# Routing of a mixture of experts: wide operations on groups of tiles, rank split by shift and mask, gathers of the uncertain slots moved into their branches

## The chip, the cores and the metric

The kernel runs on one core of a Trainium2 chip. The metric is the device time of one execution in microseconds (us). The engines are TensorE (PE, and PEld for its weight loads), VectorE (DVE), ScalarE (ACT), GpSimd (POOL) and SyncE (SP), which issues most DMAs.

## The reference

Linear attention over 4 batches, 8 heads, 768 positions and 48 dimensions gives 3,072 tokens of 384 values. Each token goes to one of 8 experts, the one with the highest logit, and the output of this expert's two layers is scaled by a gate:

```python
state = alpha[:, :, t, :, None] * state + einsum('bhd,bhe->bhde', k[:, :, t], v[:, :, t])
y[:, :, t] = einsum('bhd,bhde->bhe', q[:, :, t], state)
...
logits = x @ w_gate + modality_bias[modality_id]
e_idx = argmax(logits, axis=1)
probs = softmax(logits);  gate_w = probs[arange(N), e_idx]
for e in range(8):
    h = maximum(x[e_idx == e] @ w1[e], 0)          # 384 -> 1024
    out[e_idx == e] = gate_w[..., None] * (h @ w2[e])  # 1024 -> 384
```

## The kernel before, in words

**Attention.** The tokens are 24 tiles of 128, called chunks. A loop runs over the chunks in a software pipeline: `decay` (L229) makes the scans G and Fw on VectorE, `scale` (L254) the products kh and qh (L257, L260), `scores` (L263) the score matmuls (L269), and `combine` (L284) carries the state: t = S*G on VectorE (L292), its copy UB by ScalarE (L295), the state's matmuls kv (L301), and the output matmuls y (L314 with UB, L316 with the scores), copied to yt by ScalarE (L318). `rows` (L321) transposes yt and stores the tokens in DRAM (`xd`); `logits` (L332) does the logits of two chunks at once and adds the bias table bt (L347).

**Routing.** `route_group` (L388) runs after chunks 5, 11, 15, 17, 21 and 23, for groups of 6, 6, 4, 2, 4 and 2 tiles. Per group: the highest logit mx; per tile eq, which marks the highest logits by a descending number (L395); m2 and the one-hot oh (L397); matmuls with a triangle of ones and with all ones, which count for each token how many tokens of its expert come before it (L399 to L405, in PSUM tile rp); per tile the rank r1, as a sum over rj (L407); ohs, the running sum of oh (L412, L415); per tile hr, the rank divided by 128, as a count of thresholds not above it (hj, L417); hi (a key of expert and hr) and lo (the rest of the division); per tile OL (L423), which holds the token's number at column lo. `route_early` (after chunks 15 and 17) picks the experts of slots 0 and 1 and starts their weights and gathers. `route_end` (L524) counts the tokens of each expert (the count matmul, L529 to L531), lays out the remaining slots, and forms with OH (L558) and OL in a matmul (the table, L565) the list of tokens of each slot.

**Experts.** A slot is 256 tokens of one expert; 12 slots always exist (NS0 = 12). Weights are split into two parts for exact products (w1H, w1L, w2H, w2L, L775 and L777), as are the tokens (xL, L769) and the hidden values (hL, L802). GpSimd gathers the tokens of a slot (`gather`, L605) and their gates (`gather_gates`, L610) and scatters the results (`put`, L748). Slots 12 to 18 are uncertain: `tail(i)` (L872) enters slot i if ns > i (L874), and does a full slot if nfl > i, else one of 128 tokens (`half`). In both cases `ahead_of(i + 1)` (L866) starts weights and gathers of the next slot first. For these inputs ns is 13 and slot 12 is a half one, so slot 13 is not entered. Behind the tail a flag is tested (L908) for inputs out of range, which is not taken; then two puts write tile `of`, slot 12's result.

**Order.** Queues are in order. The order of the instructions on each engine is set when the kernel is built, by a scheduler that simulates the engines; a change of one instruction can therefore move others. An `If` that isn't taken is a jump on each engine, and the skipped side brings the engine's semaphores up to date (EVENT_SEMAPHORE, and INC_SWDGE_SEM for GpSimd's DMA queue, named ISA in the order), which on GpSimd waits for its DMAs in flight.

Of the kernel before, what the change touches and what calls it, by code (L numbers as in the profile page):

```python
# [21 lines left out]
P = 128  # L22
# [5 lines left out]
E = 8  # L28
# [3 lines left out]
NU = N // P  # L32
# [22 lines left out]
def attention_moe(ctx: ExitStack, tc: tile.TileContext, q, k, v, alpha, mid, wg, mb, w1, w2, out):  # L55
    nc = tc.nc
# [130 lines left out]
    pool.memset(ones, 1.0)  # L187
    tri = cp.tile([P, P], BF16, name="tri")
    pool.affine_select(tri, ones, [[1, P]], ALU.is_gt, 0.0, base=0, channel_multiplier=-1)
    thr = cp.tile([P, NU - 1], F32, name="thr")  # L190
    pool.tensor_scalar(thr, iof[:, 1:NU], float(P), None, op0=ALU.mult)
    onh = cp.tile([P, NU - 1], F32, name="onh")
    pool.memset(onh, 1.0)
# [138 lines left out]
    def logits(i, after=None):  # L332

        lt = ps.tile([P, 2, P], F32, name="kv")
        with issue_after(after):
            for j in range(NP):
                mark["logitst"] = pe.matmul(
                    lt[32 * j : 32 * j + 32], wgp[:, j], st[i, "yt"][:, :, j], start=True, stop=True
                )
        ls = sb.tile([P, 2, P], F32, name="lts")  # L340
        mark["xc"] = act.copy(ls, lt)
        lp = ps.tile([P, 2, P], F32, name="kv")
        for c in range(2):
            mark["logits"] = pe.transpose(lp[:, c], ls[:, c], ident)
        z = slice(i - 1, i + 1)
        vec.tensor_reduce(L[:, z], lp.rearrange("p c (j e) -> p c e j", e=32)[:, :, :E], axis=AX.X, op=ALU.add)
        vec.tensor_tensor(L[:, z], L[:, z], bt[:, z], op=ALU.add)  # L347

    def logits_pe(i, xs, pl):
        xt = ps.tile([P, ND, P], F32, name="tr", bufs=3)  # L350
        for c in range(ND):
            pe.transpose(xt[:, c], xs[:, c * P : (c + 1) * P], ident)
        xc = pl.tile([P, ND, P], F32, name="xc")
        act.copy(xc, xt)
        lp = ps.tile([P, E], F32, name="kv")
        for c in range(ND):
            pe.matmul(lp, xc[:, c], wgs[:, c], start=(c == 0), stop=(c == ND - 1))
        vec.tensor_tensor(L[:, i], lp, bt[:, i], op=ALU.add)

    mx = cp.tile([P, NU], F32, name="mx")
# [11 lines left out]
    key0 = cp.tile([P, 2], F16, name="key0")  # L373
    OHE = cp.tile([P, EARLY[-1], 2], F16, name="OHE")
    rj = cp.tile([P, E], F32, name="rj")
    hj = cp.tile([P, NU - 1], F32, name="hj")
    hr = cp.tile([P, NU], F32, name="hr")
    r1 = cp.tile([P, NU], F32, name="r1")
    lo = cp.tile([P, NU], F32, name="lo")
    OL = cp.tile([P, NU, P], F16, name="OL")  # L380
    meta = cp.tile([1, NS + 2], I32, name="meta")
    idx = cp.tile([P, NH], I32, name="idx")
# [5 lines left out]
    def route_group(t0, t1):  # L388
        n = t1 - t0
        s = slice(t0, t1)  # L390
        sh = [P, n, E]

        vec.tensor_reduce(mx[:, s], L[:, s], axis=AX.X, op=ALU.max)
        for t in range(t0, t1):
            vec.scalar_tensor_tensor(eq[:, t], L[:, t], mx[:, t : t + 1], rev, op0=ALU.is_equal, op1=ALU.mult)  # L395
        vec.tensor_reduce(m2[:, s], eq[:, s], axis=AX.X, op=ALU.max)
        vec.tensor_tensor(oh[:, s], eq[:, s], m2[:, s].unsqueeze(2).broadcast_to(sh), op=ALU.is_equal)  # L397
        rp = ps.tile([P, n, E], F32, name="rt")
        pe.matmul(rp, tri, oh[:, s], start=True, stop=False)  # L399
        for t in range(t0, t1 - 1):  # L400
            m = t1 - 1 - t
            pe.matmul(
                rp[:, t + 1 - t0 :], ones, oh[:, t].unsqueeze(1).broadcast_to([P, m, E]), start=False, stop=False
            )
        mark["rank"] = pe.matmul(rp, ones, ohs.unsqueeze(1).broadcast_to(sh), start=False, stop=True)  # L405
        for t in range(t0, t1):
            vec.scalar_tensor_tensor(  # L407
                rj, rp[:, t - t0], 1.0, oh[:, t], op0=ALU.mult, op1=ALU.mult, accum_out=r1[:, t : t + 1]
            )
        if t1 == NU and n > 1:  # L410
            vec.tensor_reduce(hsum, oh[:, t0 : t1 - 1].rearrange("p t e -> p e t"), axis=AX.X, op=ALU.add)
            vec.tensor_tensor(ohs, ohs, hsum, op=ALU.add)  # L412
        elif t1 < NU:
            vec.tensor_reduce(hsum, oh[:, s].rearrange("p t e -> p e t"), axis=AX.X, op=ALU.add)
            vec.tensor_tensor(ohs, ohs, hsum, op=ALU.add)  # L415
        for t in range(t0, t1):
            vec.scalar_tensor_tensor(  # L417
                hj, thr, r1[:, t : t + 1], onh, op0=ALU.is_le, op1=ALU.mult, accum_out=hr[:, t : t + 1]
            )
        vec.scalar_tensor_tensor(hi[:, s], m2[:, s], -float(NU), hr[:, s], op0=ALU.mult, op1=ALU.add)  # L420
        vec.scalar_tensor_tensor(lo[:, s], hr[:, s], -float(P), r1[:, s], op0=ALU.mult, op1=ALU.add)
        for t in range(t0, t1):
            vec.tensor_scalar(OL[:, t], ioh, lo[:, t : t + 1], tok[:, t : t + 1], op0=ALU.is_equal, op1=ALU.mult)  # L423

    nj = cp.tile([P, E, 2, NS0], F32, name="nj")
    nn = cp.tile([P, 2, E], F32, name="nn")
# [53 lines left out]
    def route_early(s):  # L480
# [14 lines left out]
        else:  # L495
# [28 lines left out]
    def route_end(na):  # L524
# [30 lines left out]
        for g in range(3):  # L555
            n = NU // 3
            z = slice(g * n, (g + 1) * n)
            vec.tensor_tensor(  # L558
                OH[:, z, :nh],
                key[:, :nh].unsqueeze(1).broadcast_to([P, n, nh]),  # L560
                hi[:, z].unsqueeze(2).broadcast_to([P, n, nh]),
                op=ALU.is_equal,
            )
            for t in range(g * n, (g + 1) * n):
                mark["table"] = pe.matmul(tp, OL[:, t], OH[:, t, :nh], start=(t == 0), stop=(t == NU - 1))  # L565
        for m, g in ((NS, NG), (NS + 1, E)):
            vec.tensor_scalar(meta[:, m : m + 1], beg[0:1, g : g + 1], float(na), float(NS), op0=ALU.add, op1=ALU.min)
        return places(tp, slice(z0, NH))

    ls = cp.tile([P, NU, E], F32, name="ls")  # L570
    sm = cp.tile([P, NU], F32, name="sm")
    gt = cp.tile([P, NU], F32, name="gt")

# [11 lines left out]
    def gates(t0, t1):  # L585
        z = slice(t0, t1)
        sh = [P, t1 - t0, E]
        vec.tensor_tensor(ls[:, z], L[:, z], mx[:, z].unsqueeze(2).broadcast_to(sh), op=ALU.subtract)
        act.activation(ls[:, z], ls[:, z], AF.Exp)
        vec.tensor_reduce(sm[:, z], ls[:, z], axis=AX.X, op=ALU.add)  # L590
        vec.tensor_scalar(sm[:, z], sm[:, z], 1e-9, None, op0=ALU.add)
# [159 lines left out]
    def experts(ahead):  # L751
# [114 lines left out]
        def ahead_of(i):  # L866
            if i < NS:
                weights(i, i % 2)
                gather(i)
                gather_gates(i)  # L870

        def tail(i):  # L872
            if i < NS:
                with tc.If(ns > i):  # L874
                    if i > NS0:
                        prep(i)
                    with tc.If(nfl > i) as full:
                        ahead_of(i + 1)
                        act.copy(XH[i % 2], xf)
                        vec.tensor_tensor(XL[i % 2], xf, XH[i % 2].bitcast(F32), op=ALU.subtract)  # L880
                        slot(i)
                    with full.Else():
                        ahead_of(i + 1)
                        half(i)
                    tail(i + 1)
# [59 lines left out]
```

## Time and profile before

| | |
|---|---|
| median of 3 runs | 447.57 us (447.39 to 449.25) |
| profiled execution | 447.26 us, of which the span of the trace is 445.4 |
| mean granted TensorE clock | 0.965 |
| PE | busy 396.4 us (89% of the span) |
| DVE | busy 276.3 us (62%) |
| ACT | busy 234.7 us (53%) |
| POOL | busy 139.6 us (31%) |

Attention and the routing beside it take the first 192 us or so, a transition with the last routing group and the first slot reaches to 211, and the slots run from there to 423. Times of rows are counted from the span's start. In a row of the timeline `[1.84 <-ACT UB L295]` says that the engine stood idle for 1.84 us and that the end of ScalarE's copy UB at line 295 released it. Shapes are partitions x elements.

### The profile page before, as it was taken

The page shows a single profiled execution, that of the slowest core. Times are in us where ns is not written, and L with a number is a line of the kernel's source. Part 1 is how long each engine was busy: PE and PEld are TensorE (multiplying, and loading weights), DVE is VectorE, ACT ScalarE, POOL GpSimd, SP SyncE. Part 2 cuts the span into 40 slices and gives each one's busy share as a digit, 9 for nine tenths or more (in the row PEclk, how much of TensorE's full clock was granted, in tenths as well). Part 3 has the DMA queues.
Part 4 walks back from the last instruction along what each step waited for, and adds up shares of the span by engine and source line. Part 5 has one row for each costly group of instructions (what it writes and reads, how often), then busy time and mean ns, then how long its engine had stood idle before and what let it go on. Part 6 is the DMA issues. An engine that isn't in the chain of part 4 may idle for free. (4 is left out here: it accounts for less than half of the span.)

```text
span 445.4 us, 9742 instructions
## 1 busy us (share of the span) xinstructions
PE 396.4 (89%) x3658; PEld 361.0 (81%) x3658; DVE 276.3 (62%) x659; ACT 234.7 (53%) x441; POOL 139.6 (31%) x181
## 2 busy tenths in 40 slices
PE   3999987999799899969999999999999999999900
PEld 3878776877677677847999999999999999999900
DVE  7886766656957798366976575675665665621400
ACT  3577573565565545555566556565575565432400
POOL 9321121112212233400831855363253431310501
PEclk9899996999999999998999999999999999999975
DMA  8989872666557496400999596576766855840200
GB/s 153 207 184 210 180 155 56 134 136 141 110 118 155 88 351 229 166 18 1 347 383 366 187 323 220 197 239 213 257 184 198 309 177 162 292 133 2 77 11 4
DMA packets 134748, 78.80 MB, mean 177 GB/s; under 512 B 103969, under 2 KB 121438, under 8 KB 134680
## 3 DMA queue, kind: packets, MB, share of 16 engines
q1 hardware_dynamic: 130328, 67.72, 54.6%
q0 software_dynamic: 4352, 10.24, 6.4%
q8 instruction: 34, 0.56, 0.5%
q14 instruction: 34, 0.28, 0.2%
HBM read 68.49 MB, written 9.84 MB: 176 GB/s over the span
## 5 line engine op out<-in xcount | busy, mean ns | idle before, releaser
L777 DVE TENSOR_TENSOR w2L<-w2r,w2H 128x768 fp32r<-128x768 f32 x52 | 49.4, 957 | 53.1 <-ACT w2H L775 52.8
L796 PE MATMUL tr<-xH,w1H 128*128 128x256 f32 x264 | 75.6, 286 | 0.0
L798 PE MATMUL tr<-xH,w1L 128*128 128x256 f32 x264 | 74.7, 283 | 0.0
L797 PE MATMUL tr<-xL,w1H 128*128 128x256 f32 x264 | 74.6, 283 | 0.0
L274 POOL TENSOR_SCALAR_AFFINE_SELECT scT<-scT 128x512 f32<-128x512 f32 x48 | 33.1, 709 | 123.7 <-ACT scT L273 123.7
L817 PE MATMUL sc<-w2H,hH 128*128 128x384 f32 x192 | 64.1, 336 | 0.0
L818 PE MATMUL sc<-w2L,hH 128*128 128x384 f32 x192 | 63.7, 334 | 0.0
L775 ACT CAST w2H<-w2r 128x768 fp32r<-128x768 f32 x52 | 42.6, 832 | 37.4 <-PE sc L819 33.3
L819 PE MATMUL sc<-w2H,hL 128*128 128x384 f32 x192 | 62.2, 334 | 0.0
L748 POOL DMA_INDIRECT out_dram<-os,odx x24 | 26.6, 1109 | 98.7 <-ACT os L821 66.8
L777 DVE TENSOR_TENSOR w1L<-w1r,w1H 128x768 fp32r<-128x768 f32 x44 | 41.8, 958 | 20.7 <-ACT w1H L775 20.7
L775 ACT CAST w1H<-w1r 128x768 fp32r<-128x768 f32 x44 | 36.3, 833 | 31.8 <-PE tr L797 26.5
L796 PEld LDWEIGHTS tr<-xH,w1H 128*128 128x128 f32 x264 | 50.5, 191 | 0.1
L797 PEld LDWEIGHTS tr<-xL,w1H 128*128 128x128 f32 x264 | 50.5, 191 | 0.0
L798 PEld LDWEIGHTS tr<-xH,w1L 128*128 128x128 f32 x264 | 50.5, 191 | 0.0
L605 POOL DMA_INDIRECT xg<-xd,idx x28 | 34.5, 1232 | 37.9 <-DVE vals L474 21.7
L316 PE MATMUL y<-scT,vt 128*64 128x128 f32 x384 | 43.2, 284 | 0.2
L314 PE MATMUL y<-qh,UB 128*64 128x128 f32 x320 | 39.6, 289 | 3.7 <-ACT UB L295 3.7
L610 POOL DMA_INDIRECT gg<-gd,idx x28 | 32.1, 1147 | 24.4 <-DMA gd<-gs 16.4
L269 PE MATMUL sc<-qh,kh 48*128 48x128 f32 x384 | 30.8, 296 | 9.8 <-DVE qh L260 9.8
L257 DVE TENSOR_TENSOR kh<-tr,G 128x512 f32<-128x512 f32 x24 | 16.5, 686 | 35.8 <-PE tr L224 35.8
L802 DVE SCALAR_TENSOR_TENSOR hL<-tr,hH 128x512 fp32r<-128x512 f32 x48 | 32.8, 684 | 9.2 <-ACT hH L800 9.1
(220 smaller groups left out, 800.5 us busy)
## 6 DMA issues: line engine op xcount, KB each, us to landing
w1r<-in_moe_w_dram SPq DMA_DIRECT2D x28, 768.0 KB, 5.0
w2r<-in_moe_w_dram SPq DMA_DIRECT2D x28, 768.0 KB, 6.7
nat_a<-in_alpha_dram SPq DMA_DIRECT2D x24, 192.0 KB, 3.0
nat_k<-in_k_dram SPq DMA_DIRECT2D x24, 192.0 KB, 3.4
nat_q<-in_q_dram SPq DMA_DIRECT2D x24, 192.0 KB, 3.4
vt<-in_v_dram SPq DMA_DIRECT2D x24, 192.0 KB, 3.4
xd<-xs SPq DMA_DIRECT2D x24, 192.0 KB, 2.6
xg<-xd,idx POOLq DMA_INDIRECT x28, 6.0
```

The source lines that it names most:

```text
L274: pool.affine_select(s, s, [[0, NP], [1, P]], ALU.is_ge, 0.0, base=0, channel_multiplier=-1)
L314: pe.matmul(y[r, j], U[:, j, g], qh[:, j], start=True, stop=False)
L316: pe.matmul(y[r, j], vt[:, 2 * j + g], sc[g][:, j], start=(c == 0), stop=True)
L605: pool.indirect_dma_start(xg[i % NX][:, u], None, xd[0:rows], ix, bounds_check=rows - 1, oob_is_err=False)
L775: act.copy(hi, src)
L777: vec.tensor_tensor(lw, src, hi.bitcast(F32), op=ALU.subtract)
L796: pe.matmul(hp[:, z], wH[:, d, fs], xH[:, d], start=(d == 0), stop=False)
L797: pe.matmul(hp[:, z], wH[:, d, fs], xL[:, d], start=False, stop=False)
L798: pe.matmul(hp[:, z], wL[:, d, fs], xH[:, d], start=False, stop=(d == ND - 1))
L817: pe.matmul(op, hH[:, z, us], wH[:, z], start=(f == 0), stop=False)
L818: pe.matmul(op, hH[:, z, us], wL[:, z], start=False, stop=False)
L819: pe.matmul(op, hL[:, z, us], wH[:, z], start=False, stop=(f == NF - 1))
```

## The change

In `route_group` the operations per tile become one operation on the whole group: the bias is added once per group and no longer per pair of chunks; ls = L - mx is formed here (it was formed later, for the gates) and eq compares it with zero; rank, products and sums are one operation each; hr and lo come from the whole-number rank by a shift by 7 and a mask by 127 in place of the thresholds; OL is one comparison of the column number with lo, and holds 1 in place of the token's number. The token's number (tok16) is multiplied into OHE and OH instead. In `tail` the gathers of slots 13 and up move from the slot ahead into the slot's own branch; those of slot 12 and all weight loads stay where they were.

```diff
@@ logits, logits_pe
-        vec.tensor_tensor(L[:, z], L[:, z], bt[:, z], op=ALU.add)
...
-        vec.tensor_tensor(L[:, i], lp, bt[:, i], op=ALU.add)
+        vec.tensor_copy(L[:, i], lp)
@@ route_group
+        vec.tensor_tensor(L[:, s], L[:, s], bt[:, s], op=ALU.add)
         vec.tensor_reduce(mx[:, s], L[:, s], axis=AX.X, op=ALU.max)
-        for t in range(t0, t1):
-            vec.scalar_tensor_tensor(eq[:, t], L[:, t], mx[:, t : t + 1], rev, op0=ALU.is_equal, op1=ALU.mult)
+        vec.tensor_tensor(ls[:, s], L[:, s], wide(mx), op=ALU.subtract)
+        vec.scalar_tensor_tensor(eq[:, s], ls[:, s], 0.0, over(rev), op0=ALU.is_equal, op1=ALU.mult)
...
-        for t in range(t0, t1):
-            vec.scalar_tensor_tensor(
-                rj, rp[:, t - t0], 1.0, oh[:, t], op0=ALU.mult, op1=ALU.mult, accum_out=r1[:, t : t + 1]
-            )
+        vec.tensor_tensor(rk[:, s], rp, oh[:, s], op=ALU.mult)
+        with nc.allow_low_precision("whole numbers"):
+            vec.tensor_reduce(r1[:, s], rk[:, s], axis=AX.X, op=ALU.add)
...
-        for t in range(t0, t1):
-            vec.scalar_tensor_tensor(
-                hj, thr, r1[:, t : t + 1], onh, op0=ALU.is_le, op1=ALU.mult, accum_out=hr[:, t : t + 1]
-            )
+        vec.tensor_scalar(hr[:, s], r1[:, s], 7, None, op0=ALU.arith_shift_right)
+        vec.tensor_scalar(lo[:, s], r1[:, s], P - 1, None, op0=ALU.bitwise_and)
         vec.scalar_tensor_tensor(hi[:, s], m2[:, s], -float(NU), hr[:, s], op0=ALU.mult, op1=ALU.add)
-        vec.scalar_tensor_tensor(lo[:, s], hr[:, s], -float(P), r1[:, s], op0=ALU.mult, op1=ALU.add)
-        for t in range(t0, t1):
-            vec.tensor_scalar(OL[:, t], ioh, lo[:, t : t + 1], tok[:, t : t + 1], op0=ALU.is_equal, op1=ALU.mult)
+        vec.tensor_tensor(OL[:, s], over(ioh, P), wide(lo, P), op=ALU.is_equal)
@@ route_early, behind OHE = (key0 == hi)
+        vec.tensor_tensor(
+            OHE[:, :n], OHE[:, :n], tok16[:, :n].unsqueeze(2).broadcast_to([P, n, 2]), op=ALU.mult
+        )
@@ route_end, behind OH = (key == hi), three times
+            vec.tensor_tensor(
+                OH[:, z, :nh], OH[:, z, :nh], tok16[:, z].unsqueeze(2).broadcast_to([P, n, nh]), op=ALU.mult
+            )
@@ gates
-        vec.tensor_tensor(ls[:, z], L[:, z], mx[:, z].unsqueeze(2).broadcast_to(sh), op=ALU.subtract)
@@ ahead_of, tail
                 weights(i, i % 2)
-                gather(i)
-                gather_gates(i)
...
                     if i > NS0:
+                        gather(i)
+                        gather_gates(i)
                         prep(i)
```

Line numbers of the kernel after differ by a few: L399 to L405 become L404 to L410, L314 and L316 become L312 and L314, L257, L260 and L292 become L255, L258 and L290, L874 becomes L876, L908 becomes L912.

The change moves instructions at three places that the prediction speaks of: the first group, on VectorE and TensorE, the last group on VectorE, and the end on GpSimd. VectorE, first group (after chunk 5), from the one-hot oh on, before:

```order
L397 TENSOR_TENSOR oh<-eq,m_194 128x48
L239 RECIPROCAL DF_150<-amin 128x4
L306 COPY S<-kv 128x192
L414 TENSOR_REDUCE hsum<-oh 128x8
L241 SCALAR_TENSOR_TENSOR Fw<-X_148,DF_150 128x516
L257 TENSOR_TENSOR kh<-tr,G 128x512
L292 TENSOR_TENSOR t_1132<-S,G 128x192
L260 TENSOR_TENSOR qh<-tr,Fw 128x512
```

The same stretch of VectorE in the kernel after:

```order
L402 TENSOR_TENSOR oh<-eq,m_192 128x48
L236 TENSOR_SCALAR amin<-G 128x4
L418 TENSOR_REDUCE hsum<-oh 128x8
L237 RECIPROCAL DF_150<-amin 128x4
L304 COPY S<-kv 128x192
L239 SCALAR_TENSOR_TENSOR Fw<-X_148,DF_150 128x516
L290 TENSOR_TENSOR t_1708<-S,G 128x192
L255 TENSOR_TENSOR kh<-tr,G 128x512
L258 TENSOR_TENSOR qh<-tr,Fw 128x512
```

The state's product t has moved ahead of kh. TensorE in the same group, behind the rank matmuls, before (y are the outputs, sc the next chunk's scores, tr<-ident,yt the transposes of yt):

```order
L301 MATMUL kv<-vt_102,knat 64x48 x8
L314 MATMUL y<-qh,UB_158 64x128
L269 MATMUL sc<-qh,kh 128x128 x8
L314 MATMUL y<-qh,UB_158 64x128
...
L316 MATMUL y<-scT,vt_102 64x128 x2
L325 MATMUL tr<-ident,yt 128x128 x4
```

And after:

```order
L299 MATMUL kv<-vt_102,knat 64x48 x8
L312 MATMUL y<-qh,UB_158 64x128 x2
...
L314 MATMUL y<-scT,vt_102 64x128 x2
L267 MATMUL sc<-qh,kh 128x128 x8
L323 MATMUL tr<-ident,yt 128x128 x4
```

The scores have moved from the middle of the y matmuls to behind the last of them. VectorE in the last group (after chunk 23), with the names' numbers, since the weight splits w2L of slot 0 stand between; before:

```order
L396 TENSOR_REDUCE m2_194<-eq_193 128x2
L777 TENSOR_TENSOR w2L_3018<-w2r0_113,w2H_3016 128x768
L397 TENSOR_TENSOR oh_195<-eq_193,m2_194 128x16
L777 TENSOR_TENSOR w2L_3033<-w2r0_113,w2H_3031 128x768
L411 TENSOR_REDUCE hsum_197<-oh_195 128x8
L407 SCALAR_TENSOR_TENSOR rj_206,r1_209<-rt_2914,oh_195 128x8
L777 TENSOR_TENSOR w2L_3048<-w2r0_113,w2H_3046 128x768
L412 TENSOR_TENSOR ohs_196<-ohs_196,hsum_197 128x8
L777 TENSOR_TENSOR w2L_3063<-w2r0_113,w2H_3061 128x768
```

And after, where one split already stands ahead of m2:

```order
L401 TENSOR_REDUCE m2_192<-eq_191 128x2
L781 TENSOR_TENSOR w2L_2968<-w2r0_113,w2H_2966 128x768
L402 TENSOR_TENSOR oh_193<-eq_191,m2_192 128x16
L781 TENSOR_TENSOR w2L_2983<-w2r0_113,w2H_2981 128x768
L415 TENSOR_REDUCE hsum_195<-oh_193 128x8
L781 TENSOR_TENSOR w2L_2998<-w2r0_113,w2H_2996 128x768
L411 TENSOR_TENSOR rk_205<-rt_2849,oh_193 128x16
L773 TENSOR_TENSOR xL1_2943<-y_3007,xH1_2941 128x256
L773 TENSOR_TENSOR xL1_2943<-kv_3000,xH1_2941 128x512
L416 TENSOR_TENSOR ohs_194<-ohs_194,hsum_195 128x8
```

The running sum ohs has moved behind the two splits xL of slot 1's tokens. GpSimd at the end, from the loads of ns and nfl on (the two branch pairs are slots 12 and 13, xg and gg the gathers), before:

```order
L902 TENSOR_LOAD meta
L903 TENSOR_LOAD meta
L874 COMPARE_AND_BRANCH
L877 COMPARE_AND_BRANCH
L605 DMA xg_117<-xd,idx 128x384 x2
L610 DMA gg_120<-gd,idx 128x1 x2
L877 UNCONDITIONAL_BRANCH
L605 DMA xg_117<-xd,idx 128x384 x2
L610 DMA gg_120<-gd,idx 128x1 x2
L877 UNCONDITIONAL_BRANCH
L874 COMPARE_AND_BRANCH
```

And after:

```order
L906 TENSOR_LOAD meta
L907 TENSOR_LOAD meta
L876 COMPARE_AND_BRANCH
L881 COMPARE_AND_BRANCH
L881 UNCONDITIONAL_BRANCH x2
L876 COMPARE_AND_BRANCH
L609 DMA xg_117<-xd,idx 128x384 x2
L614 DMA gg_120<-gd,idx 128x1 x2
L881 COMPARE_AND_BRANCH
```

Slot 13's four gathers have moved behind the branch that tests ns > 13.

More of the change, by code (lines that the diff above doesn't have):

```diff
@@ L189, in attention_moe @@
     pool.affine_select(tri, ones, [[1, P]], ALU.is_gt, 0.0, base=0, channel_multiplier=-1)
[L190 to L193, printed above, removed]
+    tok16 = cp.tile([P, NU], F16, name="tok16")
+    pool.tensor_copy(tok16, tok)
     bt = cp.tile([P, NU, E], F32, name="bt")
@@ L375, in attention_moe @@
     rj = cp.tile([P, E], F32, name="rj")
[L376 to L379, printed above, removed]
+    rk = cp.tile([P, NU, E], F32, name="rk")
+    hr = cp.tile([P, NU], I32, name="hr")
+    r1 = cp.tile([P, NU], I32, name="r1")
+    lo = cp.tile([P, NU], I32, name="lo")
+    ls = cp.tile([P, NU, E], F32, name="ls")
     OL = cp.tile([P, NU, P], F16, name="OL")
@@ L391, in route_group, with wide, over @@
         sh = [P, n, E]
+        def wide(a, m=E):
+            return a[:, s].unsqueeze(2).broadcast_to([P, n, m])
+        def over(a, m=E):
+            return a.unsqueeze(1).broadcast_to([P, n, m])
+        vec.tensor_tensor(L[:, s], L[:, s], bt[:, s], op=ALU.add)
         vec.tensor_reduce(mx[:, s], L[:, s], axis=AX.X, op=ALU.max)
-        for t in range(t0, t1):
-            vec.scalar_tensor_tensor(eq[:, t], L[:, t], mx[:, t : t + 1], rev, op0=ALU.is_equal, op1=ALU.mult)
+        vec.tensor_tensor(ls[:, s], L[:, s], wide(mx), op=ALU.subtract)
+        vec.scalar_tensor_tensor(eq[:, s], ls[:, s], 0.0, over(rev), op0=ALU.is_equal, op1=ALU.mult)
         vec.tensor_reduce(m2[:, s], eq[:, s], axis=AX.X, op=ALU.max)
-        vec.tensor_tensor(oh[:, s], eq[:, s], m2[:, s].unsqueeze(2).broadcast_to(sh), op=ALU.is_equal)
+        vec.tensor_tensor(oh[:, s], eq[:, s], wide(m2), op=ALU.is_equal)
         rp = ps.tile([P, n, E], F32, name="rt")
@@ L568, in route_end @@
         return places(tp, slice(z0, NH))
-    ls = cp.tile([P, NU, E], F32, name="ls")
     sm = cp.tile([P, NU], F32, name="sm")
```

## The prediction

> **What bounds the kernel now.** I read the page's slices first: TensorE is busy in nearly every slice, from the first chunk to the last expert slot, so time can only be gained where TensorE stands idle, where its clock is halved, and behind its last matmul. The second view is therefore TensorE's timeline, row by row with the idle time ahead of a row and what ended it (start, duration, engine, line, operation, tiles, shapes, count). These are the idle times at the routing groups: after chunk 5 (three rows), after chunk 11 (three rows), after chunk 15 and chunk 17 (one each), after chunk 23 (two), and one ordinary chunk without routing, at 98.06.
>
> ```profile
> 66.79 0.18 PE L399 MATMUL rt<-oh,tri 128*128 128x48 bf16 x1 [0.58 <-DVE oh L397]
> 69.65 0.69 PE L314 MATMUL y<-qh,UB 128*64 128x128 f32 x2 [1.84 <-ACT UB L295]
> 76.76 0.66 PE L325 MATMUL tr<-ident,yt 128*128 128x128 f32 x4 [0.81 <-ACT yt L318]
> ...
> 98.06 1.16 PE L269 MATMUL sc<-qh,kh 48*128 48x128 f32 x16 [0.89 <-DVE qh L260]
> ...
> 115.44 0.18 PE L399 MATMUL rt<-oh,tri 128*128 128x48 bf16 x1 [0.50 <-DVE oh L397]
> 118.31 0.43 PE L314 MATMUL y<-qh,UB 128*64 128x128 f32 x2 [1.84 <-ACT UB L295]
> 122.74 0.66 PE L325 MATMUL tr<-ident,yt 128*128 128x128 f32 x4 [1.02 <-ACT yt L318]
> ...
> 152.22 1.16 PE L269 MATMUL sc<-qh,kh 48*128 48x128 f32 x16 [1.76 <-DVE qh L260]
> 166.64 1.16 PE L269 MATMUL sc<-qh,kh 48*128 48x128 f32 x16 [0.62 <-DVE qh L260]
> 198.47 0.17 PE L399 MATMUL rt<-oh,tri 128*128 128x16 bf16 x1 [1.80 <-DVE oh L397]
> 201.40 0.18 PE L529 MATMUL rt<-ohs,ones 128*128 128x8 bf16 x1 [2.17 <-DVE rj L407]
> ```
>
> All of them end on VectorE, straight or through a copy by ScalarE (UB is copied from t). So in these places VectorE is the bound, and only there does a shorter routing pay. The table by stretches then shows the clock (busy time of each engine, granted clock, DMA share): the first two stretches hold the y matmuls behind the first group, the third the same matmuls behind the second group, the last the stretch behind the last group.
>
> ```profile
> 69.24:72.65 3.41, 3.00 (x22) 2.45 (x24) 3.23 (x31) 1.40 (x4) 0.00 (x0) 0.50 0.00 0
> 72.65:76.07 3.42, 3.31 (x30) 2.90 (x26) 1.31 (x6) 0.43 (x1) 0.00 (x0) 0.50 0.02 5
> 118.30:121.72 3.42, 3.41 (x48) 2.88 (x48) 3.31 (x33) 1.13 (x4) 0.00 (x0) 1.00 0.02 5
> 202.36:205.77 3.41, 3.41 (x10) 2.70 (x9) 3.27 (x22) 2.18 (x4) 0.00 (x0) 0.50 0.02 5
> ```
>
> The idle time of the first group thus costs twice: the same work takes 69.65 to 75.95 there and 118.31 to 121.72 at full clock, 6.30 against 3.41 us.
>
> Last the end. ScalarE's last copy, of TensorE's last matmuls, is done at 423.5, yet the first put of `of` starts at 434.38. The timeline of ScalarE and GpSimd, and the rows of the branch lines L874 and L908 by engine (durations in ns, first and last start in us; a small q is the engine's sequencer), show what lies between.
>
> ```profile
> 415.67 1.66 POOL L748 DMA_INDIRECT out_dram<-os,odx  x1 [3.90 <-ACT w2H L775]
> ...
> 422.19 1.00 POOL L610 DMA_INDIRECT gg<-gd,idx  x1 [0.30 <-issue]
> ...
> 422.95 0.58 ACT L862 ACTIVATE of<-sc,gg 128x384 f32<-128x384 f32 x1 [3.55 <-PE sc L860]
> ...
> 434.38 1.02 POOL L748 DMA_INDIRECT out_dram<-of,odx  x1 [11.20 <-issue]
> ```
>
> ```profile
> L874 POOLq EVENT_SEMAPHORE  x4: 17/43/43, 421.8 to 425.4; - x4
> ...
> L874 PEldq COMPARE_BRANCH  x3: 86/190/4779, 411.1 to 425.4; - x3
> ...
> L874 POOLq INC_SWDGE_SEM  x1: 1788/1788/1788, 425.5 to 425.5; - x1
> ```
>
> ```profile
> L908 SPq EVENT_SEMAPHORE  x9: 17/17/17, 404.5 to 405.1; - x9
> L908 POOLq EVENT_SEMAPHORE  x5: 17/43/43, 430.9 to 431.3; - x5
> ...
> L908 ACTq EVENT_SEMAPHORE  x2: 17/17/17, 430.5 to 430.5; - x2
> L908 SPq COMPARE_BRANCH  x1: 45/45/45, 402.0 to 402.0; - x1
> ...
> L908 POOLq COMPARE_BRANCH  x1: 50/50/50, 427.8 to 427.8; - x1
> L908 POOLq INC_SWDGE_SEM  x1: 1761/1761/1761, 431.4 to 431.4; - x1
> ```
>
> GpSimd's chain is: four gathers for slot 13, which does not exist here, issued until 422.19; their landings, waited for at L874 until 425.4; a queue update of 1.79; the jump of L908 from 427.8 to 430.9; another update from 431.4, 1.76; the put.
>
> **The change part by part.**
>
> *Groups after chunks 5 and 11.* VectorE's order there, with durations:
>
> ```profile
> 64.11 0.92 DVE L395 SCALAR_TENSOR_TENSOR eq<-L,mx,rev 128x8 f32<-128x8 f32 x6
> ...
> 66.54 0.20 DVE L397 TENSOR_TENSOR oh<-eq,m 128x48 bf16<-128x48 f32 x1
> ...
> 67.14 1.22 DVE L241 TENSOR_TENSOR_SCAN Fw<-X,DF 128x516 f32<-128x516 f32 x1
> 68.28 0.67 DVE L257 TENSOR_TENSOR kh<-tr,G 128x512 f32<-128x512 f32 x1
> 68.86 0.35 DVE L292 TENSOR_TENSOR t<-S,G 128x192 f32<-128x192 f32 x1
> ```
>
> Six eq become one operation of 48 elements, which by the oh row (48 elements) takes about 0.2. The bias addition and ls, new ahead of it, cost about as much each, partly overlapped; m moves from behind the scan G to before it. I take oh 0.7 earlier (0.92 − 0.2 − 2 × 0.1 + 0.2 for m): the 0.58 is gone. t now stands ahead of kh: 0.58 earlier by the starts of kh and t, with the 0.7 about 1.28. UB's matmul starts at 68.4 in place of 69.65, TensorE arrives 0.58 earlier, and the wait is 1.84 − 0.70 = 1.14. The y matmuls now run in one piece, with the next scores behind them, so ScalarE's copy of yt is covered by 1.16 of matmuls and the 0.81 goes. Against that, the following chunk has Fw ahead of qh, as the ordinary chunk at 98.06: I charge its 0.89. First group: 0.58 + 1.84 + 0.81 = 3.23 of idle become 1.14 + 0.89 = 2.03: **−1.2**. Second group: 3.36 become 2.03: **−1.3**. Either end: −2.1 if the 0.89 is not paid, 0 if kh, now later, is waited for.
>
> *The clock.* The half clock from 69.24 follows a stretch of 3.41 us with 0.58 + 1.43 idle in it; the one from 202.36 follows one with 2.17. The 1.84 behind the second group lies across two stretches and halved nothing. With 1.14 left no stretch can hold 2 us: I take the whole 6.30 − 3.41: **−2.9** (0 to −2.9). [...]
>
> *Wide tail of the routing.* The rows by shape (count, busy us, mean ns):
>
> ```profile
> L423 DVE TENSOR_SCALAR OL<-ioh,lo,tok 128x128 f16<-128x128 f16 x24 | 6.3, 327 | 0.2
> L417 DVE SCALAR_TENSOR_TENSOR hj<-thr,r,onh 128x23 f32<-128x23 f32 x24 | 6.1, 255 | 0.1
> ```
>
> hj (6.1 for 24) goes for two small operations per group. OL becomes one operation per group. An operand broadcast from int32 with f16 out is in no row; the bounds are 0.95 per 768 columns (the w2L row below) and 6 × 0.327. I take 0.95. In the first two groups this stands behind t and qh, and what it saves ends in VectorE's later idle time: 0.
>
> *Groups after chunks 15 and 17.* There qh was late because of what stood ahead of it:
>
> ```profile
> 150.19 1.23 DVE L241 TENSOR_TENSOR_SCAN Fw<-X,DF 128x516 f32<-128x516 f32 x1
> ...
> 151.48 0.69 DVE L260 TENSOR_TENSOR qh<-tr,Fw 128x512 f32<-128x512 f32 x1
> ```
>
> Now qh stands ahead of Fw of the next chunk and behind only hr, lo and hi. Moving it past Fw alone gives 1.15; the four rj and hj between give more. Of 1.76 I take **−1.3** (−0.9 to −1.76); of the 0.62 after chunk 17 all, **−0.6** (0 to −0.6). The extra multiplication by tok16 in route_early is one operation of 32 or 36 elements, under 0.2, ahead of a matmul that is queued behind other work: 0.
>
> *The last group.* Here the change makes the path longer. oh now has two of slot 0's weight splits ahead of it, and the running sum ohs, for which the count matmul waits, stands behind two xL:
>
> ```profile
> 199.35 0.95 DVE L777 TENSOR_TENSOR w2L<-w2r,w2H 128x768 fp32r<-128x768 f32 x1
> ...
> 201.42 0.42 DVE L769 TENSOR_TENSOR xL<-y,xH 128x256 fp32r<-128x256 f32 x1
> 201.75 0.68 DVE L769 TENSOR_TENSOR xL<-kv,xH 128x512 fp32r<-128x512 f32 x1
> ```
>
> The rank matmul waits 1.0 longer, but the count matmul, with four splits ahead of it either way, only by the two xL and a small sum, 1.1. TensorE has two matmuls of its own between and then idles: **+1.1** (0 to +1.7). A longer idle can also halve a second stretch of 3.41, which would be 1.7 more; I charge **+0.4** for it. Behind it there are about ten first-layer matmuls of slot 0 for TensorE between the count and the table, and they cover the three added multiplications of OH by tok16. If that cover is gone, they cost up to 1.15.
>
> *The end.* The four gathers move into the body of slot 13, which is not entered. GpSimd then jumps at L874 right behind the put at 415.67 (sequencer free at about 417). With the longest jump of a row, 4.78, two updates of 1.8, the load of the flag 0.3, the longest jump again and 1.2 of issue, its put would be at 432; with its own 3.1 per jump at 429. What is late next is ScalarE: the put waits for its skip branch of L908, at 430.5. It starts 0.3 to 0.8 behind that: 431.0 against 434.38, **−3.4**. If all jumps became as short as SyncE's lone one (402.0 to 404.5), the put would be at 429 and this −5.3; if GpSimd's stay the longest, −2.4. [...]
>
> Sum: −1.2 − 1.3 − 2.9 − 1.3 − 0.6 + 1.1 + 0.4 − 3.4 = −9.2 from the profiled execution's 447.26 (the median of the runs is 447.57): 438.1. Since most bounds of the first terms lie on the side of more gain, I say **437.8**. All of TensorE's idle time behind a DVE wait carries to the end, since it stays busy from 211 to 423.
>
> **The rivals.** (a) *The clock is halved anyway*, by phase or by a new stretch behind the last group: 437.8 + 2.9 = 440.7. For it: 2.03 of idle are left near each group. Chance 0.18. (b) *The end does not shorten*: GpSimd's own jumps and updates set it, or the gathers are still reached: −0 to −2.4 instead of −3.4, 440.2 to 441.2. Against it: the gathers' landings are what the rows at L874 wait for. 0.10. (c) *Only the end arrives*: VectorE's order, not its operations, makes the waits, kh and Fw take over: 447.26 − 3.4 + 0.2 = 444.1. For it: at 98.06 an ordinary chunk waits 0.89 with no routing at all. 0.09. (d) *Slower*: the wide comparison with an int32 operand broadcast along its columns runs at several times the row's rate. Over 24 tiles it has 3,072 columns; 1.24 ns each (0.95 per 768) are assumed. If VectorE is the bound throughout, the gains of 9.5 are used up at 1.24 + 3.1 = 4.3 ns per column, and at 5.1 the kernel takes 450. The one-tile row, 327 for 128 columns, is 2.55 at worst. 0.03.
>
> **How the numbers follow.** The forecast has 0.60; its own bounds are 434.5 to 440. The range 434.3 to 443.0 takes in (a) and (b) and leaves out (c), (d) and the far ends, under 2 in 10. A difference of 0.5%, 2.2 us, is about what a measurement of this kernel can tell from none. Faster than 445.3 are the forecast, (a), (b) and most of (c): 0.93; (d) is slower: 0.03; 0.04 remain between.
>
> **What would show it.** Right: no half clock near 69; a UB wait near 1.1 at both groups and none at yt; qh's 1.76 gone; the wait ahead of the count matmul longer; no gathers behind the last put of `os`, and the final put less than 0.9 behind ScalarE's event of the flag's branch. Wrong: an OL row much over 1 us; GpSimd's event later than ScalarE's; new waits on kh in the chunks behind a group.

## The result, and the profile after

The changed kernel takes 440.64 us (median of 4 runs, 439.87 to 442.57) against 447.48 before (447.36 to 449.25): a ratio of 0.9845, with a 95% interval of 0.9805 to 0.9884. That is 6.8 us less, where the forecast of 437.8 would be 9.7 less; the time lies in the range. The profiled execution took 439.87, its span is 438.1, 7.3 below that of before.

To see where the 7.3 come from I follow points that both kernels share, mostly matmuls behind a wait. TensorE's timeline of the kernel after has these rows; the kernel before had its at 49.33, 98.06, 144.03 and 192.65, of which three were not shown yet:

```profile
49.33 1.16 PE L269 MATMUL sc<-qh,kh 48*128 48x128 f32 x16 [0.89 <-DVE qh L260]
...
144.03 1.16 PE L269 MATMUL sc<-qh,kh 48*128 48x128 f32 x16 [0.88 <-DVE qh L260]
...
192.65 0.55 PE L325 MATMUL tr<-ident,yt 128*128 128x128 f32 x3 [0.68 <-ACT yt L318]
```

```profile
49.13 1.16 PE L267 MATMUL sc<-qh,kh 48*128 48x128 f32 x16 [0.89 <-DVE qh L258]
...
66.24 0.18 PE L404 MATMUL rt<-oh,tri 128*128 128x48 bf16 x1 [0.31 <-DVE oh L402]
...
67.25 0.67 PE L299 MATMUL kv<-vt,knat 128*64 128x48 f32 x16 [0.68 <-DVE S L304]
69.02 0.43 PE L312 MATMUL y<-qh,UB 128*64 128x128 f32 x2 [1.10 <-ACT UB L293]
69.86 0.44 PE L312 MATMUL y<-qh,UB 128*64 128x128 f32 x1 [0.41 <-ACT UB L293]
...
89.46 0.65 PE L323 MATMUL tr<-ident,yt 128*128 128x128 f32 x4 [0.74 <-ACT yt L316]
...
95.90 1.16 PE L267 MATMUL sc<-qh,kh 48*128 48x128 f32 x16 [0.89 <-DVE qh L258]
...
112.92 0.18 PE L404 MATMUL rt<-oh,tri 128*128 128x48 bf16 x1 [0.23 <-DVE oh L402]
...
140.47 1.16 PE L267 MATMUL sc<-qh,kh 48*128 48x128 f32 x16 [0.89 <-DVE qh L258]
...
187.85 0.66 PE L323 MATMUL tr<-ident,yt 128*128 128x128 f32 x4 [0.68 <-ACT yt L316]
...
194.66 0.17 PE L404 MATMUL rt<-oh,tri 128*128 128x16 bf16 x1 [2.78 <-DVE oh L402]
...
197.55 0.19 PE L532 MATMUL rt<-ohs,ones 128*128 128x8 bf16 x1 [2.14 <-DVE ohs L416]
```

The end of the kernel after, in the timeline of ScalarE and GpSimd and in the rows of the flag's branch (now L912):

```profile
420.15 0.58 ACT L866 ACTIVATE of<-sc,gg 128x384 f32<-128x384 f32 x1 [3.52 <-PE sc L864]
...
427.41 0.98 POOL L752 DMA_INDIRECT out_dram<-of,odx  x1 [12.85 <-ACTq L912]
```

```profile
L912 SPq EVENT_SEMAPHORE  x9: 17/17/17, 401.9 to 402.5; - x9
...
L912 ACTq EVENT_SEMAPHORE  x2: 17/17/17, 427.1 to 427.2; - x2
L912 SPq COMPARE_BRANCH  x1: 45/45/45, 399.3 to 399.3; - x1
...
L912 POOLq INC_SWDGE_SEM  x1: 1677/1677/1677, 422.5 to 422.5; - x1
L912 ACTq COMPARE_BRANCH  x1: 50/50/50, 423.4 to 423.4; - x1
```

The stretch of a row of this table is the difference of the two points in each kernel:

| stretch | before | after | difference | forecast |
|---|---|---|---|---|
| start to the point at 49 | 49.33 | 49.13 | -0.2 | 0 |
| group after chunk 5, to 98.06 / 95.90 | 48.73 | 46.77 | -2.0 | -1.2 and clock -2.9 |
| group after chunk 11, to 144.03 / 140.47 | 45.97 | 44.57 | -1.4 | -1.3 |
| groups after 15, 17, 21, to 192.65 / 187.85 | 48.62 | 47.38 | -1.2 | -1.9 |
| last group and slots, to ScalarE's last copy, 422.95 / 420.15 | 230.30 | 232.30 | +2.0 | +1.5 |
| last copy to the first final put, 434.38 / 427.41 | 11.43 | 7.26 | -4.2 | -3.4 |
| to the end of the span | 11.02 | 10.69 | -0.3 | 0 |

The clock table of the kernel after, with the stretches at half clock (granted clock 0.50): behind the first group there is now one and not two, behind the last group two and not one.

```profile
69.94:73.35 3.41, 3.41 (x30) 3.16 (x30) 1.84 (x8) 0.70 (x2) 0.00 (x0) 0.50 0.02 5
...
196.23:199.64 3.41, 2.09 (x8) 1.73 (x9) 3.27 (x19) 0.00 (x0) 0.00 (x0) 0.50 0.00 0
199.64:203.06 3.42, 3.42 (x10) 2.70 (x9) 1.82 (x10) 2.46 (x4) 0.00 (x0) 0.50 0.02 5
```

In the first group the rank matmul still waits (0.31), a wait ahead of kv is new (0.68), and so is a second one for UB (0.41): 2.50 in place of 3.23. The group's wait for yt is gone, but one of 0.74 is new at 89.46. In the second group the rank matmul waits 0.23, and behind it stand the same three waits as in the first (0.68, 1.10 and 0.41): 2.42 in place of 3.36. VectorE's and GpSimd's timelines show what the forecast had not seen: oh takes 0.57, not 0.20, and amin 0.63, while two selects of GpSimd run, the first (shown) stretched to 1.52, the second to 66.71.

```profile
65.61 0.57 DVE L402 TENSOR_TENSOR oh<-eq,m 128x48 bf16<-128x48 f32 x1
66.11 0.63 DVE L236 TENSOR_SCALAR amin<-G 128x4 f32<-128x4 f32 x1
...
66.88 0.32 DVE L304 COPY S<-kv 128x192 f32<-128x192 f32 x1
67.12 1.22 DVE L239 TENSOR_TENSOR_SCAN Fw<-X,DF 128x516 f32<-128x516 f32 x1
68.26 0.33 DVE L290 TENSOR_TENSOR t<-S,G 128x192 f32<-128x192 f32 x1
```

```profile
64.61 1.52 POOL L272 TENSOR_SCALAR_AFFINE_SELECT scT<-scT 128x512 f32<-128x512 f32 x1 [5.43 <-ACT scT L271]
```

My theory from here: the end shortens by itself, as far as ScalarE's jumps; VectorE and GpSimd hold each other in the first two groups; the last group pays for its order on VectorE; and the clock adds or takes up to 1.7 per stretch (half of 3.41), by where a wait falls among its stretches. The experiments take these one by one. Beside them the kernel before ran from 447.0 to 454.5, so their ratios have wide intervals; I read them by the changed kernel's times (440.64, and 440.83 in the repeat) and by the stretches of their traces. A few runs at a lower clock count as slow and are left out of the ratios, among them one of four of the kernel with the gathers alone (451.0), whose other three have a median of 443.96.

### The profile page after: what moved, and what is told of

It reads as the page before. It is cut to its first block, busy times and chain, and to the rows that moved or that the text cites. A ratio compares the mean times of both kernels' runs of the same rounds, so it can differ in the third digit from the quotient of the medians.

```text
span 438.1 us, 9621 instructions
## 1 busy us (share of the span) xinstructions
PE 396.2 (90%) x3658; PEld 360.3 (82%) x3658; DVE 272.0 (62%) x548; ACT 233.7 (53%) x441; POOL 133.1 (30%) x176
## 5 line engine op out<-in xcount | busy, mean ns | idle before, releaser
L272 POOL TENSOR_SCALAR_AFFINE_SELECT scT<-scT 128x512 f32<-128x512 f32 x48 | 32.0, 689 | 120.6 <-ACT scT L271 120.6
L609 POOL DMA_INDIRECT xg<-xd,idx x26 | 31.8, 1222 | 39.9 <-DVE vals L474 24.7
L314 PE MATMUL y<-scT,vt 128*64 128x128 f32 x384 | 43.8, 286 | 0.0
L312 PE MATMUL y<-qh,UB 128*64 128x128 f32 x320 | 40.8, 287 | 3.0 <-ACT UB L293 3.0
L255 DVE TENSOR_TENSOR kh<-tr,G 128x512 f32<-128x512 f32 x24 | 16.5, 687 | 38.0 <-PE tr L222 38.0
L804 ACT ACTIVATE hH<-tr 128x512 fp32r<-128x512 f32 x48 | 28.5, 594 | 17.1 <-PE tr L802 8.7
L614 POOL DMA_INDIRECT gg<-gd,idx x26 | 29.3, 1128 | 22.2 <-DMA gd<-gs 11.6
```

What stands on the lines that cost most here:

```text
L272: pool.affine_select(s, s, [[0, NP], [1, P]], ALU.is_ge, 0.0, base=0, channel_multiplier=-1)
L312: pe.matmul(y[r, j], U[:, j, g], qh[:, j], start=True, stop=False)
L314: pe.matmul(y[r, j], vt[:, 2 * j + g], sc[g][:, j], start=(c == 0), stop=True)
```

## The experiments

**The end.** Two kernels take the change apart. The first is the kernel before with the gathers moved; the second the changed kernel with the gathers where they were.

```diff
         def ahead_of(i):
             if i < NS:
                 weights(i, i % 2)
-                gather(i)
-                gather_gates(i)
...
                     if i > NS0:
+                        gather(i)
+                        gather_gates(i)
                         prep(i)
```

> The kernel before with one part of the change: slot 13's gathers moved into its branch, routing as before. Theory (the end shortens by itself, its length is set by ScalarE's two jumps behind its last copy): the stretch from that copy's start to the first final put is 7.3 as in the changed kernel, against 11.4 before, and the time falls by 4.0 to 4.7, to about 443.1. Rival (the two parts need each other, since a front that ends earlier changes which jumps collide): a fall of 2.5 to 3.5, put at least 8 behind the copy.

Its timeline (ScalarE's last copy and the first final put):

```profile
424.12 0.58 ACT L862 ACTIVATE of<-sc,gg 128x384 f32<-128x384 f32 x1 [3.55 <-PE sc L860]
...
431.50 0.98 POOL L748 DMA_INDIRECT out_dram<-of,odx  x1 [12.99 <-ACTq L908]
```

7.38 between them, released by ScalarE, against 11.43 before and 7.26 in the changed kernel: the theory. The time, 443.96 (ratio 0.9883, 0.9788 to 0.9978; the median of all four runs is 445.19), is 3.5 below the 447.48 of before and near the expected 443.1, but says less: in the trace ScalarE's last copy comes 1.2 later than before, with one stretch of half clock more.

> The change without its last part: slot 13's gathers stay ahead of the branch, routing as in the changed kernel. Theory (front and end are independent): from ScalarE's last copy to the first final put 11.2 to 11.6, and a time 4.2 to 4.5 above that of the changed kernel, about 445. Rival: under 3 above.

The same two rows of this kernel:

```profile
424.43 0.58 ACT L866 ACTIVATE of<-sc,gg 128x384 f32<-128x384 f32 x1 [3.52 <-DMA xg<-xd,idx]
...
435.64 1.02 POOL L752 DMA_INDIRECT out_dram<-of,odx  x1 [10.93 <-issue]
```

11.21, nearly as before. It takes 445.93 (444.32 to 448.79; ratio 0.9916, 0.9886 to 0.9946), 5.1 to 5.3 above the changed kernel where 4.2 to 4.5 were expected. Moving the gathers takes about 4 from the end with either routing (11.43 to 7.38, and 11.21 to 7.26), so there the two edits are independent, and the smaller one brings more than half of the result. What the routing alone is worth is less certain: 1.6 against the first 447.48 of before, 3.5 against the 449.43 that before took beside this run.

**VectorE and GpSimd in the first two groups.** First an order: the scan G of chunks 10 and 16 stands behind oh.

```diff
-        vec.tensor_tensor(oh[:, s], eq[:, s], wide(m2), op=ALU.is_equal)
+        mark["oh", t0] = vec.tensor_tensor(oh[:, s], eq[:, s], wide(m2), op=ALU.is_equal)
...
         if s < NU:
-            decay(s)
+            with issue_after({10: ("oh", 0), 16: ("oh", 6)}.get(s)):
+                decay(s)
```

> The changed kernel with one order forced: in the groups after chunks 5 and 11 the next chunk's scan G stands behind the one-hot oh on VectorE. Theory (oh and amin take 0.57 and 0.63 in place of 0.20 and 0.17 because GpSimd's selects, themselves held by the scan, run beside them, and this also keeps back the copy S): oh takes 0.20 again, the wait ahead of the rank matmul goes, S is about 0.5 earlier, t over 1.0 earlier, the waits of 0.68 and 1.10 shrink to under 0.7 together; 1.2 to 1.8 per group, and up to 1.7 more if the half clock near 70 goes: 436 to 438.5. Rival (the shape or the operand types make oh slow): oh stays at 0.57, and the time falls by less than 1.

VectorE's timeline in its first group, and the wait of TensorE that is left ahead of kv:

```profile
65.79 0.21 DVE L402 TENSOR_TENSOR oh<-eq,m 128x48 bf16<-128x48 f32 x1
65.92 1.66 DVE L232 TENSOR_TENSOR_SCAN G<-X,DR 128x516 f32<-128x516 f32 x1
...
67.63 0.40 DVE L236 TENSOR_SCALAR amin<-G 128x4 f32<-128x4 f32 x1
67.95 0.34 DVE L304 COPY S<-kv 128x192 f32<-128x192 f32 x1
...
68.33 0.36 DVE L290 TENSOR_TENSOR t<-S,G 128x192 f32<-128x192 f32 x1
...
69.20 1.22 DVE L239 TENSOR_TENSOR_SCAN Fw<-X,DF 128x516 f32<-128x516 f32 x1
```

```profile
68.35 0.67 PE L299 MATMUL kv<-vt,knat 128*64 128x48 f32 x16 [1.00 <-DVE S L304]
```

oh is short, and now G is the one held (1.66 against 1.22 elsewhere). The rank wait and the UB waits are gone, but S is behind G and amin, and kv waits 1.00 for it, more than the 0.68 that I expected to shrink. The edit also moved more than it named: the scheduler put Fw behind t and kh (69.20), where the changed kernel has it ahead of t, so the UB waits did not go by the selects' hold alone. From 50.34 to 138.16, the points before the scores of the ordinary chunks, it takes 87.82 against 91.34 in the changed kernel: 2.4 less in the first group (0.8 of it waits, the rest one half-clock stretch less) and 1.1 less in the second (1.0 of it waits). The time is 437.40 (436.73 to 438.03; ratio 0.9715, 0.9655 to 0.9776), as the theory said in total, with less of it from the waits than I had expected (1.2 to 1.8 per group).

Then the same with the order kept and the other engine taken away:

```diff
             act.copy(s, pp[g])
-            pool.affine_select(s, s, [[0, NP], [1, P]], ALU.is_ge, 0.0, base=0, channel_multiplier=-1)
+            if i not in (8, 14):
+                pool.affine_select(s, s, [[0, NP], [1, P]], ALU.is_ge, 0.0, base=0, channel_multiplier=-1)
```

> The changed kernel without GpSimd's selects of the scores of chunks 8 and 14, the two that run beside the groups after chunks 5 and 11 (the scores of these two chunks keep their upper half); VectorE's order is that of the changed kernel. Theory (these selects hold oh and amin): oh takes 0.20 and amin 0.17, S and t come 0.8 earlier, the waits ahead of rank, kv and y in each of the two groups fall from 2.2 to 2.5 to under 1.2; 2 to 3 less in all, up to 1.7 more by the clock. Rival (something else on VectorE or the shapes): oh stays at 0.57, nothing moves by over 0.3.

```profile
66.69 0.18 DVE L403 TENSOR_TENSOR oh<-eq,m 128x48 bf16<-128x48 f32 x1
66.81 0.17 DVE L236 TENSOR_SCALAR amin<-G 128x4 f32<-128x4 f32 x1
```

```profile
67.53 0.67 PE L300 MATMUL kv<-vt,knat 128*64 128x48 f32 x16 [0.27 <-DVE S L305]
69.31 0.43 PE L313 MATMUL y<-qh,UB 128*64 128x128 f32 x2 [1.10 <-ACT UB L294]
```

oh and amin are short again with no other change ahead of them on VectorE: the selects are what holds them. The waits of the two groups fall from 2.50 and 2.42 to 1.78 each (0.27 + 1.10 + 0.41), not to the 1.2 that the theory had: the hold costs 0.7 in the first group and 0.6 in the second, and the wait of 1.10 for UB stays; Fw still stands between S and t. (Without the selects the scores of two chunks keep their upper half, the values are others, and more slots run, so only the first 120 us of this kernel, and not its 554.39 us, can be compared.)

**The last group.** First its count without the running sum:

```diff
-        if t1 == NU and n > 1:
+        if t1 == NU and n > 2:
...
+        if na:
+            pe.matmul(cnt, ones, oh[:, NU - 2], start=False, stop=False)
         mark["count"] = pe.matmul(cnt, ones, oh[:, NU - 1], start=False, stop=True)
```

> The changed kernel with the count of the last group formed from the one-hots of its two tiles directly, by one more small matmul, so that it no longer waits for the running sum ohs behind the two splits xL. Theory (the order in the last group costs 1.0 of TensorE's time by that wait): the wait ahead of the count falls from 2.14 to about 1.1 and the time by 1.0 (439.6), by up to 2.7 if one half-clock stretch goes with it. Rival (the path to the table sets the end of this stretch, the wait is hidden): under 0.3, since the idle time comes back ahead of the key or table matmuls.

```profile
198.78 0.17 PE L532 MATMUL rt<-ohs,ones 128*128 128x8 bf16 x1 [1.07 <-DVE rk L411]
```

The wait falls from 2.14 to 1.07 as expected. The stretch from 190.16 to ScalarE's last copy at 420.28 is 2.2 shorter than in the changed kernel, 1.07 by the wait and the rest by one half-clock stretch. The time, 440.12 (438.71 to 442.45; ratio 0.9787, 0.9713 to 0.9861), shows only 0.5 to 0.7 of it: in the profiled execution another half-clock stretch had come behind the second group.

Then the splits of slot 0. The kernel of the next expectation puts all of its VectorE work (hidden values hL and weights w2L) behind the last operation of the layout, and slot 1's tokens ahead:

```diff
-        vec.tensor_scalar(diag[:, 1], ident[:, :NH], kc[:, 1:2], None, op0=ALU.mult)
+        mark["diag"] = vec.tensor_scalar(diag[:, 1], ident[:, :NH], kc[:, 1:2], None, op0=ALU.mult)
...
         def slot(i):
-            layer1(i)
-            if i + 1 < NS and i < NS0:
+            early = ahead and i == 0
+            if early:
+                prep(1)
+            with issue_after("diag" if early else None):
+                layer1(i)
+            if i + 1 < NS and i < NS0 and not early:
                 prep(i + 1)
```

> The changed kernel with slot 0's hidden-value and weight splits on VectorE behind the last routing group's operations, and slot 1's tokens prepared ahead of slot 0's first layer. Theory (the 4.9 of idle time around the last group are VectorE's queue, and the half clock behind it follows from them): the waits ahead of rank and count fall to under 0.7 together, a new one of 1 to 2 appears ahead of the key matmul, the half clock near 197 shrinks to one stretch or none: 435 to 438. Rival (the splits are needed at once by slot 0's second layer): TensorE waits there instead, the time stays within 1 of 440.6 or rises.

```profile
205.93 0.55 PE L800 MATMUL tr<-xH,w1H 128*128 128x256 f32 x1 [2.58 <-DVE hL L806]
```

The time is 438.98 (438.41 to 440.8; ratio 0.9751, 0.969 to 0.9813), between the ranges of the two theories. The waits ahead of rank and count fall from 4.92 to 0.78, but 0.66 and 2.58 come back where TensorE's next PSUM buffers wait for hL to be read, and behind them two stretches of half clock from 205.43. Both theories had a part.

So the last kernel lets hL go and delays only the weight splits, one behind the layout and three behind the last multiplication of OH ahead of the table. It has slot 1's tokens first, as the kernel above, and the order of oh and G of the third experiment; only the new lines are shown:

```diff
...
-                w2s.append(split("w2", W2[:, 2 * j : 2 * j + 2]))
+                with issue_after(("OHm" if j else "diag") if plain else None):
+                    w2s.append(split("w2", W2[:, 2 * j : 2 * j + 2]))
```

> The kernel of e3, and in the last group slot 0's weight splits behind the layout (the first behind the last diag, the other three behind the last multiplication of OH), slot 1's tokens prepared first; the hidden-value splits stay free, since TensorE waited 2.5 for them in e5. Theory (both corrections act in their own places and add up): the waits ahead of rank and count, 4.9, fall to about 1; one new wait of up to 1 ahead of the key or the second layer; 437.4 less 2 to 4.5: 433 to 435.5. Rival (what is saved ahead of the count comes back ahead of slot 0's second layer): 436.5 to 438.

TensorE's timeline, and the clock behind the last group:

```profile
190.79 0.17 PE L404 MATMUL rt<-oh,tri 128*128 128x16 bf16 x1 [1.25 <-DVE oh L402]
...
191.38 0.17 PE L532 MATMUL rt<-ohs,ones 128*128 128x8 bf16 x1
```

```profile
193.00:197.00 4.00, 4.00 (x20) 3.42 (x20) 3.75 (x16) 4.00 (x8) 0.00 (x0) 1.00 0.00 0
```

It takes 431.57 (430.99 to 432.77), a ratio of 0.9588 (0.9549 to 0.9627) to the kernel before: 9.1 below the changed kernel, 5.8 below the one with the order alone, and faster than I had expected (433 to 435.5). Of 4.92 in waits 1.25 are left, the count does not wait at all, and no stretch up to ScalarE's last copy is at half clock. From the transposes ahead of the last group (185.55) to that copy (412.02) it takes 226.47 against 232.30 in the changed kernel: 3.2 less of idle time, and 2.7 less of TensorE's busy time, as the two stretches of half clock are gone. How much the delayed splits and how much the earlier tokens brought, no run separates.

**The clock.** The changed kernel once more, as it is:

> The changed kernel once more, nothing changed. Theory (the stretches of half clock lie on a grid of 3.41 whose phase is another in each execution, so which idle time halves the clock is partly chance): the same idle times within 0.1 in the same places, but the half-clock stretches behind the groups in another number or place; 439 to 442.6. Rival (the clock follows the idle time alone): the same three stretches behind the first and last groups.

It took 440.83 (440.46 to 441.11; ratio 0.9795, 0.9744 to 0.9846), 8.6 below the 449.43 of the kernel before beside it, with waits at the same places, within 0.3, and the same three stretches of half clock behind the groups (one at 70.49, two from 196.78). Behind the groups the rival held in this pair. But at the first chunk the changed kernel had a stretch at half clock (from 11.9) and its repeat had none. And the kernel with the gathers alone, whose routing is that of before, has one half-clock stretch behind the first group where before had two, and one behind the second group (from 118.06) where before had none, with the same wait of 1.84 behind the second group in both: before it lay across two stretches (split at 117.03, TensorE busy for 2.34 and 2.13 of them), here all of it lies in one (busy for 1.57). So in this pair the wait is the same and where the stretches lie is not. Stretches just ahead of a possible half-clock one show the margin; the first two are of the kernel before, the next of the kernel with the gathers alone (with the stretch that followed), the last two of the changed kernel:

```profile
65.83:69.24 3.41, 1.38 (x27) 0.97 (x25) 3.41 (x11) 1.15 (x3) 1.40 (x2) 1.00 0.86 173
195.53:198.95 3.42, 1.62 (x13) 1.19 (x11) 3.15 (x10) 3.04 (x5) 0.00 (x0) 1.00 0.00 0
```

```profile
114.65:118.06 3.41, 1.57 (x28) 1.27 (x30) 3.41 (x14) 1.04 (x3) 0.05 (x1) 1.00 0.57 113
118.06:121.47 3.41, 3.41 (x36) 3.19 (x34) 3.21 (x27) 0.70 (x2) 0.00 (x0) 0.50 0.02 5
```

```profile
66.52:69.94 3.42, 1.23 (x22) 0.82 (x22) 3.42 (x11) 1.18 (x3) 0.19 (x1) 1.00 0.64 128
114.31:117.72 3.41, 1.90 (x35) 1.54 (x32) 3.41 (x13) 1.54 (x5) 0.00 (x0) 1.00 0.32 65
```

With TensorE busy for 1.38, 1.57 and 1.23 of 3.41 the next stretch ran at half clock, with 1.62 and 1.90 it did not. These five would put a bound between 1.57 and 1.62, but two runs have a case against it: the kernel with the routing alone, 1.84 busy and then half (first two rows), and the repeat at its first chunk, 1.47 busy and then full clock (last row):

```profile
65.71:69.13 3.42, 1.84 (x31) 1.43 (x29) 3.42 (x8) 0.82 (x3) 1.62 (x2) 1.00 0.96 212
69.13:72.54 3.41, 2.74 (x22) 2.34 (x24) 3.27 (x12) 1.88 (x5) 0.00 (x0) 0.50 0.02 4
...
9.05:12.46 3.41, 1.47 (x14) 1.48 (x16) 3.34 (x7) 0.71 (x2) 1.48 (x4) 1.00 1.00 193
```

So in these rows half clock followed 1.23 to 1.84 of busy time and full clock 1.47 to 1.90; what else enters stays open.

## Why the prediction was right, and where it was off

The range held and the sign was right; the forecast was 2.8 too hopeful, and its sum (438.1 against the profiled 439.87) 1.8. That the time lies almost on rival (a)'s 440.7 is chance: half of the clock's gain came, another term failed, and the end gave 0.8 more than its term. By its own steps:

- *The end, -3.4:* right in mechanism, measured -4.2. GpSimd is done with its queue's update at 424.2 (422.5 and 1.68) and waits for ScalarE's skip branch, whose event at 427.1 releases the put 0.3 later; the lower of the two latencies that I had (0.3 to 0.8) was the right one; and ScalarE's own way from its copy to that event shrank from 7.6 to 7.0.
- *First group, -1.2:* failed, 0: 3.23 of idle became 2.50, and 0.74 is new at 89.46. I had t come 1.28 earlier; it came 0.60 earlier (68.26 against 68.86), and 0.28 of that is a lead that VectorE already had at the scan before (62.18 against 62.46). The step that failed is that oh is 0.7 earlier, "the 0.58 is gone", and t with it. oh does start 0.65 earlier against that scan, but VectorE's durations were taken as fixed, while GpSimd's selects, in the same microseconds, hold oh and amin (0.57 and 0.63, against 0.18 and 0.17 in the kernel without the selects). In the kernel before the hold fell on amin alone (0.42), in its successor on both. Counted from that scan, t comes 0.32 earlier than before with the selects and 1.13 earlier without them. Without them the rank matmul no longer waits and the first wait for UB is 1.10 where 1.14 was forecast, but a second one (0.41) and the one for S (0.27) remain. The 0.89 charged to the next chunk's qh did not come.
- *Second group, -1.3:* measured -1.4, right by luck: the waits of the stretch fell by 0.7 only, since the same hold acts here (oh takes 0.57 and amin 0.63 again). The other 0.7 is TensorE's busy time, most of it in the score matmuls (7.7 before, 7.0 after, for the same 96); why is open.
- *The clock, -2.9:* half right. One of two stretches went, about -1.7 in the first group. The condition "with 1.14 left no stretch can hold 2" failed with the group's waits: 2.19 of idle stood in the stretch before 69.94, and one of the signs of being right, no half clock near 69, failed.
- *Groups after chunks 15 and 17, -1.9:* qh's waits of 1.76 and 0.62 went as said, and 0.94 came at the next chunk for 0.53 before. That makes -2.0 (1.76 + 0.62 + 0.53 - 0.94 less), and leaves 0.7 to the measured -1.2 that the waits do not explain: TensorE's busy time in this stretch grew by 1.0 for the same 584 matmuls, with no wait shown. This stays open.
- *The last group, +1.1 and +0.4:* right in place and mechanism. The wait ahead of rank grew by 0.98 (1.80 to 2.78) and the count came 0.95 later; its own wait did not grow (2.17 to 2.14), though a longer one was among the signs of being right. Freed of the sum behind the two xL, it is 1.07 shorter. The second half-clock stretch that I had priced at 0.4 was there in full and cost about 1.0, since TensorE was busy for 2.09 of it.

Of the rivals, (a) came in part: one stretch of half clock stayed behind the first group and one was added behind the last. (b) is out, since the end shortened by 4.2; its lower bound was also miscounted, as 437.8 + 1.0 is 438.8 and not 440.2. (c) names what happened in the first group, where the waits kept their sum, but not the rest. (d) is out: OL takes 0.95 for 768 columns, as assumed. One reading of the first view was wrong and cost nothing: the two waits for yt end on ScalarE's copy of TensorE's own y, and not on VectorE.

## What to carry to other kernels

In this kernel shortening VectorE's queue paid where a wait of TensorE ended on it (the 1.76 and 0.62 ahead of two chunks' scores went), and an operation there cost more than its row elsewhere said (oh 0.57 beside a select, 0.20 before): look at what GpSimd does in the same microsecond before taking a duration from a table. When operations get fewer, look at what the scheduler puts in their place: here four weight splits of a slot that had time stood ahead of the operation that TensorE waited for, and moving them, with slot 1's tokens first, took another 5.8, nearly as much as the change itself (6.8). A gather for a branch that is mostly not taken belongs into the branch where the skipped side waits for it, as here: in the kernel before, slot 13's last landing and the end of GpSimd's wait at L874 were both at 425.4, and moving the gathers took about 4 from the end; what that costs when the branch is taken, no run here shows.

## What the runs showed of the hardware

- Beside a select of GpSimd some operations of VectorE took longer. In the first group of the changed kernel oh took 0.57 and amin 0.63; without the two selects oh took 0.18 and amin 0.17. Where oh began 0.01 or 0.02 ahead of a select, it was short: 0.21 from 65.79 (select from 65.80) in the third experiment, 0.20 from 66.54 (select from 66.56) in the kernel before.
- In the first group the scan G and a select begin within 0.14 of each other in three runs. In the kernel before, G from 64.95 took 1.23 and the select from 64.89 took 1.72; in the changed kernel, G from 64.47 took 1.22 and the select from 64.61 took 1.52; with G behind oh, G from 65.92 took 1.66 and the select from 65.80 took 0.69. The median of the changed kernel's 48 selects is 0.63, the mean of its 24 scans G 1.23. What decides which of the two takes longer is not shown.
- In the traces of before and after TensorE's granted clock changed only at points that are whole multiples of 3.413 apart: in the kernel before half clock begins at 11.21, 69.24 and 202.36, which are 17 and 39 times 3.413 apart, and in the changed kernel at 11.91, 69.94 and 196.23, 17 and 37 times. Of the stretches above, those with TensorE idle for 1.84, 2.03 and 2.19 were followed by half clock, those with 1.80 and 1.51 were not, and one with 1.58 was; at the first chunk of the repeat one with 1.94 was not. No bound on the idle time sorts them all.
- In the kernel after, the update of GpSimd's DMA queue on the skipped side of the flag's branch takes 1.68, and the jump, from an engine's compare to its first event behind it, 2.6 on SyncE (399.3 to 401.9) and 3.7 on ScalarE (423.4 to 427.1).
